# A written order of 3,557 steps, written anew: pooled attention and a two-layer MLP on one core

## The chip, the core and the metric

The kernel runs on one core of a Trainium2 chip. The core has five engines that run side by side, each through its own instruction list in order: TensorE (PE in the profile, with its weight loads as PEld), VectorE (DVE), ScalarE (ACT), GpSimd (POOL) and SyncE (SP), which here only issues DMA transfers. Engines wait for each other through semaphores. The metric is the device time of one execution, in microseconds (us), from its start to its end.

## What is computed

The reference pools the queries by two, runs an ordinary softmax attention for 4 batches of 8 heads (1152 keys, 576 pooled queries, head size 64), and sends the result, as 2304 tokens of 512 numbers, through two dense layers with a leaky ReLU between them:

```
q_pool = q.reshape(B, H, S // 2, 2, D).mean(axis=3)
scores = (1 / sqrt(D)) * q_pool @ k.T
attn   = exp(scores - max) / (sum + 1e-9)
x      = (attn @ v), heads side by side       # 2304 x 512
h      = x @ w_in                             # 512 x 2048
out    = maximum(0.01 * h, h) @ w_out         # 2048 x 512
```

The inputs q, k and v are 32-bit floats; the two weight matrices come as 64-bit floats.

## The kernel before

The work is cut into 3,557 steps, each of one to some tens of instructions on one engine, named by their function and their place: `qk` 9 2 is the third piece of the first score product of head 9. There are 32 heads and, for the dense layers, 9 blocks of 256 tokens.

**One head** goes through this chain. The keys are loaded and turned over on TensorE (`load_k`, `k_tr`), and split into a rounded part by ScalarE (`k_hi`) and a rest by VectorE (`k_lo`); the queries are loaded into one buffer that all heads share (`load_q`, four DMAs), summed in pairs on GpSimd (`q_sum`), turned over and split likewise. `qk` computes rough scores, and `vmax` (line 476, on VectorE) takes their maxima out of the accumulation banks; a bank pair is free for the next product only when its `vmax` is done. `vneg`, `m_tr`, `m_cp` and the DMA step `m_dma` (line 496, tile mt) turn the maxima into a row. `qkt` (line 511) computes the exact scores minus the maximum in nine pieces; two bank pairs take turns, and each is freed by its `exp` on ScalarE (line 515). `pv` multiplies with the values, GpSimd adds up the sums (`esum`, line 525), and `norm` copies the result out of its bank into one of two buffers x1, on ScalarE or VectorE. The sums go the long way round: `r_cp`, the DMA step `r_fold` (four DMAs), `r_inv` on VectorE, the DMA steps `r_row` and `r_wide`, the multiplication `scale` on GpSimd (line 591) and the DMA step `x_out` (line 597, into xd). The buffer x1 of head 8 is the one of head 6, so `norm` 8 waits until the DMAs of `x_out` 6 have landed.

**The weights** come in 32 pieces of 128 x 512. The 64-bit numbers are made into 32-bit ones by `w_f32` in three steps: step 0 on ScalarE (line 619), step 1 on VectorE (line 622, a shift) and step 2 on VectorE (line 625, a shift of one SBUF operand, or-ed into a second one). `w_hi` and `w_lo` then split each piece. All this lies between 41 and 300 us, while heads 2 to 15 are at work. The dense layers (`l1`, `post`, `l2`, and for the later blocks a scheme with fewer products, `g_...`, `l2s`, `o_mix`) fill TensorE beside the later heads and alone at the end.

**What sets the order.** The string ORDER has one letter for each step; `run` goes through it, and each letter takes the next step of its family. So each engine's instruction list is the order of the letters. While `run` goes through the letters, it keeps a reckoning of when each engine is free, from prices written at each `step`. The reckoning chooses two things only: which engine does a step that may go on either of two, and which of several free buffers it takes. `lock=True` in a step on VectorE or GpSimd makes the reckoning hold the two engines apart: such a VectorE step is not begun there before GpSimd is done with its own, nor the other way round. Prices come from `dve`, `act`, `gp` and the like, functions of the number of columns: `dve(512, 2)` is 0.40 us and `dve(512)` 0.66 us. Neither the prices nor the locks put any instruction into the kernel.

Of the kernel before, what the change touches and what calls it, by code (L numbers as in the profile page):

```python
# [18 lines left out]

ND = 3  # L20
# [27 lines left out]
    "43)-244355BB%-43!4.3.4(*+3,53+6,-A.443-../7433B45)0631A4DDD9-E8(EE*6.-!4+,2+),-..BCCF#BCCA$:6%3CF(-34;8-..433!"
    "-.44.53/&-53<55GH440.31-F-4A73.3C9-544.G23.5-H45.553-4=:3.G4&*+.;D,#$+34>6<3,4E&DD/3704AEF35%-1-643HF?.9-84B)E"
    ".3-.2B3(4453-G35.-:.454.A.3/!4=*+,)#$H;5%+A364,#$%5>3D3447B0G!31<E9?CFF-4-6G82..-.G34BA3-3-43..44-3=3../:5*H4;"  # L50
    "5++C3,5>64(CC60DA41-,3-DDEF?EE.8.4-.33<#5)B=2&445H!3-45F7A$.3*+4(+6>-,5,-..?95%A6583F-4.7934.3B/:40-B;GGDD133."
    "-#)4433&$.!-42<3.4%43-3!43.-.4B455.5/A3*+,#6G6=:U;+5$C554>C,0%33A<14A-(74E35.45342H-335).-44&33=49*?55+.-(+,F."
    ":64->-,H3..587G3?443./06D1D4E;EE3A-F39F844&!G)2-343..-3-44G3.34F55<U:*++.D;=B(,,3CC>64AG<?653E&)5A-48=5344B-#."
    ".3*./$(%+>DE,?7401#2D-ER696$!+.3A8),%AB-34-4334:4..-34.-.34-5B(555555;-...A3S4&/7T3U39B<-40*).4+,+1FC,&--F-VVV"
    "VV..V-W...6FGCCG2/:U03G3=C14B4#;<(3356DDEEDE44X3$3F4554734!%3>G2=#B49$&DEC>34536?4A%53*4538H-+4.Y,+6:,33-;455A"
    "7.H3-4V?V49-8.-..U5VVV)<5-AUF3C.V4BVV.GC/01=U3-DVV24E!VHFV3>W646?GH5X3W3:.DE-U484-33.U-4U4.35455;<3*#4V.VVVV$+"
    "+%YV,,3-FF55.GXWG(XA4-V&..YVVVVV/D0EA-!=WB3124.34#-U63.$554%5>C3F-H?46F73.9-434B5G34HD8BD5:.-3-43E4..).3*Z/ZYZ"
    "+FUECCC4&HGZZZZZZG;+DEFF,ZZ[VBUV<VA,GVVVZGB3DDEUE5A=550WZV1VCFGFGCZVXZDE4XYZ52HVVV>&36WU[4?3FGBD-E3.54X463548Y"
    "3U479A:;34(F3G--VCVDVVVV<EZWYXYZZF=4ZZZZ..G-)5--ZZZZZ.Z..3[!.>?(/01*4ZZZ5+5255+,,#55553A$!4%[634-347.3349RS#T-"
    "$%648.3)3UU4U-U-.VVV5555VUVVVVV:VVVWVVVUU.54U3W*&AX+V(+VVYAZ5]W&ZXYX4YVVVV,,A-)-345..VVWZ./&;Z03<XY-!.1-4.ZZZ]"  # L60
    "2=-.*>6+,+,34ZUU-3.[347(634-3?9448-:;<55.U3434=../35555036124>4733#44A9$336%4434-?ZV:85.)5555---VV.Z&(;V&V.V.*"
    "++-.,,-.Z./<Z=>)ZZZWAZ[304!X5531#34A$24356%3443*4+?+73-5Y,,6(5)4394.-38-43..43-.534!4-UUVV:;VVVVVU55VVVV5A-UUA"
    "WVW..5X.VVVVYVVWUARX/#Y012UUX3YZZZZZZZZ$6[344S%354*34<=T6>535+U+?3,,454789&-3VV-4-.(..-VV!ZVUV.A:Z#WA$3;-.Z4Z)"
    "555--.Z.ZZVV%.34<-/01V(ZVV.V[3-.6W=>?42343-4753.!3-U4&.63-55.49U43.435:;<4/5*85555)]535013442=76>93++,3X44,#$:"
    "3*+A,+%6,54X-?-YYAVVVVVV5.;53<8W4.-.34!-555334#4.-.A-Z$.VX.A%UYUZV/V3-&(&.VVVZ4W-.=-.0Z5XZZY)ZZ1-553556]45[.23"
    "3-4.743434-../601334UU4>9*33+(44)6+34,5,55555?234*+8733,6+4554343!:;<=4>,#$93ZVVVVA4%--.V.UV?ZZ8--WX.-YUV.&VV."
    "VV!Z3-#$4..VW/55AAZU55Z0%13XY(--..)4VVZVVV52U3!45-Z[V-3.6W:3;<=.-.4344&73#*45$+U3+6>9%AX43?4,,-3A85434.!-3:./."
    "0Y1;#(-4.7ZV9VVV$%V--..2555555:3VZ<=ZZWXYZZZZ6);-<4[34.334*UA3+6+U,,44R-=34553>5?475..U/013!3>A8ST-54462.343?-"
    "693.44:34;-558.555]-334.-4(3U34-VVVV.)..A/V<&V5=&(74W3*+4+5056619,2,3344#$>34?:)8X*(AA55ZUU5Z)Z5;V5%!++,,AVZ3-"
    "<Z-43Z..-4--.ZZ.VVVV-WU[3.3.#4.Y43/!$0VV4555VVVV31=4-W%6234X>3.74-55534934&6?3.5X8-344UU.-3.3-4534-VVVVVYVWVVY"  # L70
    "..VZZ.5555Z#U/U54*++0A$VXVUYVW5ZZZ:;1A,ZZ%ZZZZZZZZ,II<2L[A6NP-JK[M3374OQ4II.3&3-46359=>.-4XN34?84-345553555.45"
    "5.-Y3.-VV:&.JV.P4VVVWXUU5YU/01UV;OL2VVVVVVVVVWVVW364343463XX344QK<79M3I3=>R?SU87443344U6IP6TVVUVVVUVVVVNJYYKOL"
    "QV:;VMI55ZVUVVUVVVZZZ5UUVVVVVVIPR<ZVZZ^Q95UNZ:5[UVVLUVVV555VV7IIMUU^Z_LMZZOZZZPQV^V=UZVZ]]V_VVVVVVJK>SJU9I:`?a"
    "`a[^__8VVUVVUUUbIbNONOJ`;;TV^_VV`<<VVVaKVVVaUILMbI^b`a_UU^=V>V=VVVVVVUVV`PaV^VUVVVU>b?KQIILMVLMJKVNO^JKPUUQNOb"
    "^PVVVVVVVQV?VVUR___`ab`abcbccbbS^^^`TUUa_VVVVVUcUVVVV^VVVVb`VUU^aV^VUUVVVVVVVVVVVU__bUcccVUVVVV_Vc`V_Va_^_UUbV"
    "`UaVVVVbV``aVVa`VbVbUU`aabb^^VVVbVVV^bb^^]d_U__URVVVVVcc_ccccU`aVUUVVVST`VVVVVVcbUUUc`UVVVVVVVVaab^`a^VVVVUVVV"
# [1001 lines left out]
```

## Time and profile before

| | us |
|---|---|
| three runs of the kernel before | 897.91, 898.41, 903.2; median 898.41 |
| the profiled execution | 897.51 |
| its span, from the first to the last instruction | 895.7 |
| TensorE busy | 861.3 |
| VectorE, GpSimd, ScalarE busy | 524.2, 494.3, 390.4 |

The span is 1.8 us shorter than the profiled execution; what lies around it is the same for any order of the work. A row of the trace gives the start of a group of like instructions in us from the start of the span, how long the group lasted, the engine, the line, the operation and its operands, how many instructions it holds, and in brackets the idle time of the engine before it and what ended that.

### The profile page before, as it was taken

How to read it: one execution, taken by the hardware profiler on the slowest of the kernel's cores; microseconds unless marked ns; L12 is line 12 of the kernel's file. 1: busy time of each engine (PE TensorE's matmuls, PEld its weight loads, DVE VectorE, ACT ScalarE, POOL GpSimd, SP SyncE). 2: the span in 40 equal slices, each digit the busy share in tenths (PEclk: the TensorE clock that was granted, in tenths of full speed). 3: DMA queues.
4: the chain of work that ended last, by engine and by line, in shares of the span. 5: the costliest groups of instructions: out<-in, count | busy, mean ns of one | idle time of the engine just before them, and what ended most of it. 6: DMA issues, size and time to landing. Idle time of an engine off the chain costs nothing.

```text
span 895.7 us, 19761 instructions
## 1 busy us (share of the span) xinstructions
PE 861.3 (96%) x7736; PEld 693.0 (77%) x7736; DVE 524.2 (59%) x813; ACT 390.4 (44%) x706; POOL 494.3 (55%) x400
## 2 busy tenths in 40 slices
...
GB/s 207 214 175 209 171 166 152 173 203 202 256 245 195 107 252 172 115 194 160 131 146 110 146 130 150 129 191 109 117 180 247 205 247 256 197 267 177 242 143 48
DMA packets 107309, 159.74 MB, mean 178 GB/s; under 512 B 25856, under 2 KB 74304, under 8 KB 107216
## 3 DMA queue, kind: packets, MB, share of 16 engines
...
q8 instruction: 61, 1.00, 0.5%
...
## 4 chain that ended last, share of the span: by engine, by line
PE 81%; DMA 6%; DVE 6%; SPq 2%; issue 2%; ACT 2%; POOL 0%; DVEq 0%; ACTq 0%; POOLq 0%
PE banks L690 22%; PE banks L511 17%; PE banks L537 13%; PE banks L781 11%; PE banks L461 4%; PE banks L822 3%; PE banks L824 3%; PE banks L823 3%; DVE stat L476 2%; DMA rt<-rs 2%; PE banks L553 1%; DMA ws<-wd 1%; DMA raw<-in_moe_w_in_dram 1%; PE banks L548 1%; SPq L571 1%
## 5 line engine op out<-in xcount | busy, mean ns | idle before, releaser
L476 DVE TENSOR_REDUCE stat<-banks 128x1 f32<-128x1024 f32 (+3 forms) x224 | 217.6, 1005 | 113.5 <-PE banks L461 96.7
L515 ACT ACTIVATE e<-banks 128x576 f32<-128x576 f32 x234 | 148.2, 650 | 136.8 <-PE banks L511 120.6
L690 PE MATMUL banks<-xb,ws 128*128 128x256 f32 x1344 | 176.4, 285 | 0.3 <-DMA ws<-wd 0.2
L690 PEld LDWEIGHTS banks<-xb,ws 128*128 128x128 f32 x1344 | 167.4, 190 | 10.2 <-issue 4.8
L525 POOL TENSOR_TENSOR sm<-sm,e 128x576 f32<-128x576 f32 x119 | 171.0, 1454 | 3.4 <-ACT e L515 2.0
L511 PE MATMUL banks<-qh,ka 64*128 64x288 f32 x1152 | 146.5, 330 | 5.9 <-DVE stat L476 4.0
L537 PE MATMUL banks<-e,vv 128*64 128x288 f32 x936 | 139.5, 411 | 0.1
L511 PEld LDWEIGHTS banks<-qh,ka 64*128 64x128 f32 x1152 | 93.9, 191 | 52.6 <-issue 18.6
L537 PEld LDWEIGHTS banks<-e,vv 128*64 128x64 f32 x936 | 70.0, 136 | 50.6 <-issue 7.0
L511 PE MATMUL banks<-mt,hot 64*128 64x288 f32 x576 | 89.8, 297 | 2.2 <-DMA mt<-ms 2.2
L511 PE MATMUL banks<-ql,ka 64*128 64x288 f32 x576 | 88.1, 296 | 0.0
L591 POOL TENSOR_TENSOR x<-x,rs 128x288 f32<-128x288 f32 x32 | 27.0, 846 | 99.9 <-DMA rs<-rd 86.5
L461 PE MATMUL banks<-ka,qh 64*128 64x512 f32 (+1 forms) x320 | 69.4, 445 | 6.4 <-ACT ka L256 2.2
L511 PEld LDWEIGHTS banks<-mt,hot 64*128 64x128 f32 x576 | 58.1, 189 | 3.3 <-DMA mt<-ms 3.1
L781 PE MATMUL banks<-wo,gg 128*128 128x256 f32 x340 | 60.3, 282 | 0.0
L411 POOL TENSOR_TENSOR qs<-qn 112x384 f32<-112x384 f32 x32 | 32.9, 1029 | 49.3 <-DMA qn<-in_q_dram 22.7
L525 POOL TENSOR_TENSOR sm<-e 128x576 f32<-128x576 f32 x32 | 46.1, 1441 | 24.3 <-ACT e L515 24.3
L511 PEld LDWEIGHTS banks<-ql,ka 64*128 64x128 f32 x576 | 57.3, 190 | 0.0
L432 DVE SCALAR_TENSOR_TENSOR ql<-banks,qh 64x288 fp32r<-64x288 f32 x66 | 29.9, 453 | 46.1 <-ACT qh L429 45.3
L703 POOL TENSOR_TENSOR gg<-g,gg 128x512 fp32r<-128x512 f32 x32 | 41.8, 1311 | 22.1 <-DVE gg L256 11.6
L822 PE MATMUL banks<-wo,gg 128*128 128x512 f32 x128 | 53.3, 416 | 0.0
L824 PE MATMUL banks<-wo,gg 128*128 128x512 f32 x128 | 50.9, 398 | 0.0
...
## 6 DMA issues: line engine op xcount, KB each, us to landing
...
qn<-in_q_dram SPq DMA_DIRECT2D x128, 72.0 KB
...
```

Source lines behind the costliest of these rows:

```text
L411: ENG[e].tensor_tensor(out=qs[hd][:n], in0=a, in1=b, op=ALU.add)
L461: nc.tensor.matmul(p[:n, x, :KW], lhsT=qh[hd][r, o:o + n], rhs=kh[r, :KW], start=True, stop=True)
L476: nc.vector.tensor_reduce(out=d, in_=p, axis=AX.X, op=ALU.max)
L511: nc.tensor.matmul(p[:, x, :HW], lhsT=w[r], rhs=m[r, hf * HW:(hf + 1) * HW], start=(n == 0), stop=(n == 3))
L515: nc.scalar.activation(out=ex[hd, u], in_=sps.pop((hd, u))[:, :, :HW], func=AF.Exp)
L525: ENG[e].tensor_tensor(out=o, in0=a, in1=b, op=ALU.add)
L537: nc.tensor.matmul(p[64 * hf:64 * hf + 64, :HW], lhsT=vv[hd][:, t, :], rhs=probs(hd, t, hf), start=(t == 0), stop=(t == KT - 1),)
L690: nc.tensor.matmul(p, lhsT=wst[i, f][:, a, c, :], rhs=xx[i][x][:, c, :], start=(n == 0), stop=(n == 3 * KC - 1))
L703: ENG[e].tensor_tensor(out=t[:, 1], in0=gf.pop((i, fp)), in1=f32(t[:, 0]), op=ALU.subtract)
L781: nc.tensor.matmul(o, lhsT=g[i, p][:, a], rhs=w[:, x], start=(p == 0 and n == 0 and half == 0), stop=(p == FH - 1 and n == 2), skip_group_ ...
L822: nc.tensor.matmul(p, lhsT=gh, rhs=wo[f][:, 0], start=(f == hf * FH), stop=False)
L824: nc.tensor.matmul(p, lhsT=gl, rhs=wo[f][:, 0], start=False, stop=(f == hf * FH + FH - 1))
```

## The change

The change has three parts. First, the whole string ORDER is another one, of the same 3,557 letters, so that every engine's instruction list is in another order. Second, some prices and locks of the reckoning are others: step 1 and step 2 of `w_f32` are reckoned at 0.78 and 1.2 us, the middle step of `post` at 0.75 us on VectorE, each without a lock; step 0 of `w_f32` has 0.06 us more; and a TensorE step that has to wait for more than 1 us in the reckoning is reckoned 1.2 us longer. Third, the `vmax` steps of head 1 now name the step `zeros`, which clears their tile on GpSimd, as one they depend on. A constant W0 is added that nothing reads. Four lines are added, so that line 476 of before is line 480 after, 622 is 626 and 625 is 629.

```diff
 ORDER = (
-    "()*+,++!+,,,!@B(B)#$--%#$.-..*--..-.+.!+,B/0(%)1A-*+,.+B-!.-CCCC2.,3A-34,--.4.34#3../&&3$40A453-(1#%-..B4A3$53"
     ...
+    "!#$%()*++++!#,,,-$%,.-.--..@B()*++B-!-.(A--)..,/01BC..--*,(C2.C.+,+,3434!-.3#)-43$.&.3/440AA3%A1-.B#55-.4!5353"
     ...
 )
@@
-        end = self.free[e] = at + s.eng[e]
+        free, end = self.free[e], at + s.eng[e]
+        self.free[e] = end
         if e == "PE":
+            if at > free + 1.0:
+                end = self.free[e] = end + 1.2
@@
-                step(vmax, hd, y[2], ..., deps=[("qk", hd, n)])
+                step(vmax, hd, y[2], ..., deps=[("qk", hd, n)] + ([("zeros", hd)] if 0 < hd < len(mts) else []))
@@
-        step(w_f32, i, 0, eng={"ACT": act(512)}, deps=[("w_load", i)])
-        step(w_f32, i, 1, eng={"DVE": dve(512, 2)}, lock=True, deps=[("w_f32", i, 0)], takes=[("raw", [("w_lo", i)])])
-        step(w_f32, i, 2, eng={"DVE": dve(512)}, lock=True, deps=[("w_f32", i, 1)])
+        step(w_f32, i, 0, eng={"ACT": act(512) + 0.06}, deps=[("w_load", i)])
+        step(w_f32, i, 1, eng={"DVE": 0.78}, deps=[("w_f32", i, 0)], takes=[("raw", [("w_lo", i)])])
+        step(w_f32, i, 2, eng={"DVE": 1.2}, deps=[("w_f32", i, 1)])
@@
-                step(post, i, fp, 1, eng={"DVE": dve(512, 2), "ACT": act(512)}, lock=True, deps=[("post", i, fp, 0)])
+                step(post, i, fp, 1, eng={"DVE": 0.75, "ACT": act(512)}, deps=[("post", i, fp, 0)])
```

**Place 1: VectorE, from the maxima of head 6 to those of head 7** (stat is written by `vmax`, neg by `vneg`, ql is the query's rest, raw a piece of the weights, rt the sums). Before:

```order
L476 TENSOR_REDUCE stat_66<-banks 64x1
L479 TENSOR_REDUCE neg_68<-stat_66 128x5
L576 TENSOR_REDUCE rt<-rt 96x6
L577 RECIPROCAL rt<-rt 96x6
L432 SCALAR_TENSOR_TENSOR ql<-banks,qh 64x288
L622 TENSOR_SCALAR raw<-raw 128x512
L432 SCALAR_TENSOR_TENSOR ql<-banks,qh 64x288
L622 TENSOR_SCALAR raw<-raw 128x512 x2
L625 SCALAR_TENSOR_TENSOR raw<-raw 128x512 x3
L476 TENSOR_REDUCE stat_67<-banks 128x1 x4
```

With the change:

```order
L480 TENSOR_REDUCE stat_66<-banks 64x1
L626 TENSOR_SCALAR raw<-raw 128x512
L629 SCALAR_TENSOR_TENSOR raw<-raw 128x512
L580 TENSOR_REDUCE rt<-rt 96x6
L581 RECIPROCAL rt<-rt 96x6
L436 SCALAR_TENSOR_TENSOR ql<-banks,qh 64x288
L483 TENSOR_REDUCE neg_68<-stat_66 128x5
L626 TENSOR_SCALAR raw<-raw 128x512 x2
L436 SCALAR_TENSOR_TENSOR ql<-banks,qh 64x288
L480 TENSOR_REDUCE stat_67<-banks 128x1 x3
```

Six steps on weights stood in a body between `vneg` 6 and the first `vmax` of head 7; two shifts stand there now, another pair stands ahead of `vneg`, and the second steps of the two shifts come after the maxima of head 7.

**Place 2: SyncE, from the maxima's row of head 9 to `x_out` 6** (mt is `m_dma`, rd `r_row`, rs `r_wide`, rt `r_fold`, qn `load_q`, xd `x_out`). Before:

```order
L496 DMA mt_73<-ms 1x5x128 x2
L580 DMA rd_84<-rt 96x6
L674 DMA ws<-wd_111 128x1024
L571 DMA rt<-rs 48x1x6 x4
L584 DMA rs<-rd_84 64x288 x2
L608 DMA raw<-in_moe_w_in_dram 128x4x128
L395 DMA qn_70<-in_q_dram 48x3x128 x4
L441 DMA ql<-ql 64x288 x2
L580 DMA rd_85<-rt 96x6
L597 DMA xd_74<-x_2107 64x288 x2
```

With the change:

```order
L584 DMA rd_84<-rt 96x6
L500 DMA mt_73<-ms 1x5x128 x2
L588 DMA rs<-rd_84 64x288 x2
L399 DMA qn_70<-in_q_dram 48x3x128 x4
L451 DMA vv<-in_v_dram 128x576
L644 DMA wd_116<-ws 128x1024
L575 DMA rt<-rs 48x1x6 x4
L601 DMA xd_74<-x_1648 64x288 x2
L601 DMA xd_74<-x_2067 64x288 x2
```

`x_out` 5, which stood five rows above this piece, now stands right ahead of `x_out` 6, and `load_q` and `r_fold` stand ahead of both. On ScalarE `norm` 7, which waits for the one, and `norm` 8, which waits for the other, now have a single `exp` between them.

**Place 3: SyncE, from the start.** Before:

```order
L395 DMA qn_70<-in_q_dram 48x3x128 x4
L366 DMA kn<-in_k_dram 128x576
L367 DMA kn<-in_k_dram 128x64
L366 DMA kn<-in_k_dram 128x576
L367 DMA kn<-in_k_dram 128x64
```

With the change:

```order
L370 DMA kn<-in_k_dram 128x576
L371 DMA kn<-in_k_dram 128x64
L399 DMA qn_70<-in_q_dram 48x3x128 x4
L370 DMA kn<-in_k_dram 128x576
L371 DMA kn<-in_k_dram 128x64
```

The keys of head 0 now go ahead of its queries. Further on, the fourth `load_q` stands ahead of the `m_dma` of head 0, where it stood behind it before.

## Rows read from the trace of the kernel before

**Rows 1.** The page: the span, and TensorE's busy time.

```profile
span 895.7 us, 19761 instructions
PE 861.3 (96%) x7736; PEld 693.0 (77%) x7736; DVE 524.2 (59%) x813; ACT 390.4 (44%) x706; POOL 494.3 (55%) x400
```

**Rows 2.** Windows: stretch, length; busy us (instructions) of five engines; granted clock; DMA.

```profile
0.00:45.00 45.00, 32.74 (x305) 23.44 (x305) 31.79 (x50) 21.90 (x40) 14.92 (x21) 1.00 0.70 211
45.00:270.00 225.00, 209.20 (x2142) 148.41 (x2141) 159.07 (x219) 134.37 (x249) 159.94 (x123) 0.96 0.65 196
270.00:895.70 625.70, 619.35 (x5294) 521.10 (x5292) 333.29 (x544) 234.17 (x418) 319.43 (x256) 1.00 0.55 170
```

**Rows 3.** TensorE's timeline: its waits of over 1 us from 45 to 270 us.

```profile
71.31 0.28 PE L485 MATMUL banks<-ident,neg 64*128 64x64 f32 x2 [1.10 <-DVE neg L479]
...
105.08 0.49 PE L461 MATMUL banks<-ka,qh 64*128 64x512 f32 x1 [1.24 <-ACT x L256]
108.53 0.84 PE L511 MATMUL banks<-qh,ka 64*128 64x288 f32 x4 [2.96 <-DVE stat L476]
...
143.72 0.40 PE L511 MATMUL banks<-mt,hot 64*128 64x288 f32 x1 [1.42 <-DMA mt<-ms]
...
173.49 0.43 PE L464 MATMUL banks<-ka,qh 64*128 64x128 f32 x4 [3.03 <-ACT x L256]
...
266.27 0.39 PE L420 MATMUL banks<-ident,qs 48*128 48x48 f32 x6 [1.73 <-DVE stat L476]
```

**Rows 4.** Windows, as rows 2: the five stretches of half clock.

```profile
106.79:113.60 6.81, 5.07 (x44) 4.16 (x48) 4.56 (x5) 2.41 (x5) 4.53 (x4) 0.50 0.78 259
...
144.30:147.74 3.44, 3.18 (x24) 3.18 (x26) 1.15 (x1) 1.43 (x3) 1.55 (x2) 0.50 0.86 282
...
175.05:178.46 3.41, 3.41 (x40) 1.84 (x36) 3.13 (x7) 1.38 (x4) 1.10 (x1) 0.50 0.77 229
...
195.50:198.95 3.45, 3.45 (x18) 3.45 (x17) 3.26 (x3) 1.14 (x3) 2.59 (x3) 0.51 0.85 289
...
267.21:270.60 3.39, 3.39 (x10) 2.62 (x9) 2.60 (x5) 3.35 (x7) 1.30 (x1) 0.50 0.95 364
```

**Rows 5.** VectorE's timeline, ahead of the waits at 108.53 and 266.27 us.

```profile
101.78 5.44 DVE L625 SCALAR_TENSOR_TENSOR raw<-raw 128x512 uint32<-128x512 uint32 x3
107.25 3.49 DVE L476 TENSOR_REDUCE stat<-banks 128x1 f32<-128x1024 f32 x3
...
262.14 2.85 DVE L625 SCALAR_TENSOR_TENSOR raw<-raw 128x512 uint32<-128x512 uint32 x1
```

**Rows 6.** Groups of VectorE by shape: count | busy us, mean ns | idle before.

```profile
L625 DVE SCALAR_TENSOR_TENSOR raw<-raw 128x512 uint32<-128x512 uint32 x32 | 39.0, 1235 | 0.5
...
L622 DVE TENSOR_SCALAR raw<-raw 128x512 uint32<-128x512 uint32 x32 | 24.1, 773 | 13.8 <-POOL wo L637 8.7 <-POOL ws L637 4.6 <-issue 0.5
```

**Rows 7.** Lines 625 and 622: ns of one, least/median/most.

```profile
L625 DVE SCALAR_TENSOR_TENSOR raw<-raw x32: 659/693/4234, 42.5 to 299.8; 128x512 uint32<-128x512 uint32 x32
L622 DVE TENSOR_SCALAR raw<-raw x32: 381/427/1651, 41.5 to 298.9; 128x512 uint32<-128x512 uint32 x32
```

**Rows 8.** GpSimd's timeline beside the row of 101.78 us in rows 5.

```profile
101.78 1.57 POOL L411 TENSOR_TENSOR qs<-qn 112x384 f32<-112x384 f32 x1 [3.24 <-DMA qn<-in_q_dram]
...
104.67 1.40 POOL L525 TENSOR_TENSOR sm<-e,gg 128x576 f32<-128x576 f32 x1
```

**Rows 9.** SyncE's timeline: DMA issues, start and length of the issuing.

```profile
1.19 1.84 SPq L395 DMA_DIRECT2D qn<-in_q_dram  x4
3.08 0.44 SPq L366 DMA_DIRECT2D kn<-in_k_dram  x1
...
18.47 1.60 SPq L496 DMA_DIRECT2D mt<-ms  x2
...
138.27 3.52 SPq L395 DMA_DIRECT2D qn<-in_q_dram  x4
...
170.33 1.11 SPq L597 DMA_DIRECT2D xd<-x  x2
```

More of the change, by code (lines that the diff above doesn't have):

```diff
@@ L17 @@
 DRAM = bass.MemoryType.DRAM
+W0 = 5
 ND = 3
@@ L46 @@
 ORDER = (
-    "()*+,++!+,,,!@B(B)#$--%#$.-..*--..-.+.!+,B/0(%)1A-*+,.+B-!.-CCCC2.,3A-34,--.4.34#3../&&3$40A453-(1#%-..B4A3$53"
[L48 to L76, printed above, removed]
@@ L77 @@
-    "UVV__RS_b`aVUVbbUVV`U_a^b^_^`VVaVTUUUb`aVVVVVVVVb^ddcbbccc_b__VVVVUVV`aV`UUVc^^cccV_Ub_VVUVVVVVVVU`VabVVV^`aUU"
-    "VVVVUUbVVVV^V`VabVVa`aUVV_`b_b`aaVd^^U_`VVbVbbb^^_b`dUVVUUV^VVVVVVUVcccccaabUVVVVb^UVVUVVVV__`V`_a_ccb^c_ab`ab"
-    "`^_a`a`abbbdddcbbbbccbbbbbcccbbbccddd"
+    "!#$%()*++++!#,,,-$%,.-.--..@B()*++B-!-.(A--)..,/01BC..--*,(C2.C.+,+,3434!-.3#)-43$.&.3/440AA3%A1-.B#55-.4!5353"
+    "$42%43-43434-BB(..3&*455++34,,A536-&34D45DD)5.-.7.354EE-B3/.64A0193-8B.*4(+6#+FA,,--C$C2)EBC..634-%3438-4.354:"
@@ new lines @@
+    "!;3..-/0341-7.&.<-4F9.33-4A45.G53B-2B434-3.3545#3.4*().DE++4=,G6/C,:;$3&43>4%5F7A013--D4EC.6!934!-.34<?8.2B-.H"
+    "343:-43-3.4*.AH#4=.+$,55555G+%(A3,/;FFAG<64D#$E33>754-4!%9-0.163F55CCC-.?4G348.-.H2343-3G-...44)=!B33*436+DE+4"
+    ">:64;H,/C01(DA<-?D,83--.55555..F5434&3)=#423-$6A%-..4*>-H..+6+,7E(F,393?BA-4GC87&3B43)/B9:.0-4D4!1GD32543.4-3."
+    "#43;-&3.<$4%43-4.3-34.545*+.E,H+#,3($556/4=53%4AE3EA4-016FFFU!:.->)B55534-723.53.-94G43434.*+3+4C-;(?BA<.,,863"
+    "3-.B44G33:&.A5G555/=;4A)74DE0->3<1-2..963F44--CC6=3.4.(D3&H*34DG>:EE4F3+??;!,63+,84-D83<)4A.-43.3.GD/445#55*++"
@@ new lines @@
+    ",UEF70$16=(5A#$,B%GE>-2%.-633.?&98-.-4344)5553.-A4!33.-..R4(-4U.3S4A7-T93.5:3-.-44*BVV)FFGVVG./B:V++C&,0D1B5E5"
+    "-2;,V66;CCCW.3F344H-.345G<3./D<4#0&AA13$437=34=5>9X5%E>!3D4#4234F36$%434*H3BG:;+5,6455-?DU3?ECC8+,48U79-3.C4-V"
+    ".<VVF5H3.Y-E4(VVV-.U3=-V5A45GFGW!VVA3.../H04VD1)VV3H2-EB4>?663W34XUU.XDEUUD4-85.-343-4334554555..#*V(VV++,A$YE"
+    "Y,VVCV3-%.-FGVVVFCWGX..!V/4VV0-W.1Y33#4&&H$4-.FD2B6%BX3553C4-E6B4C.D-34.B37493455555-HE.534343-ZZZZZZFFGGGCDDD"
+    "C:EEE:.BZZZ;5AHZFFF.GZZZZUG[VVVUD4VEH3<U/05F)CGGZ1Z[4VU=2DEFVUVVVVVB>V*WX++YG3W,6453;34X4,5A-C536DE34Y344?8<57"
@@ new lines @@
+    "B3&.-.V=U>VZV4VVVZC3-YFG9?WZDEZZ.-48AX-Y-FGRZ:!(;.)<ZZZZZZZ=5.*../++#S(0T)51ZZ!A>$Z52[,,6%34555555[&-347UU.334"
+    "4?#3$%946833-44-VVVVUVVUVVVVV..UU---WVVVV.VVXWAV:]YX.U../3505W*ZXUY;VZYVVZV1+V+V(4A,-,.-WXY.3ZZ&4ZZZ-<&2.3465["
+    "U35=>5435-)4!557933?U.4*+64+83,3-5544:;,.-3437.<U3=A.49/A0(1>46)6234#$3%?ZZZ:-!4A8;-..-.ZZ<ZZ&Z-[3=434.*+,>555"
+    "55U3-V?(V+VVUVVVVVUU),4VWV5555V.W-3X43..#4/013$43465*2%3Y+,+,63434A873A-43X94-4.3455534.:Y-3-.VVVVVVV.UA-;-!.W"
+    "XVVV4<5VVW355Y()#=../0ZZ$Z&Z%XYZZ1UZRZ>62[35S443743*+,4+A,3T634?5535()9-!8U.-:;<U44VVAVV&VV5555-.W=X>.--A&ZZ.Z"
@@ new lines @@
+    "ZZVZ.3-#$.4Z./ZVV01%3554--[UUVVVW(..36234434-7.35549-.63?-83-44UU:...343*/455!35501+;5+3XYY72<=44A)6&U,,6334#$"
+    "4%9>VV?VV8!-VVVV5*+-.34+AAV,5,AVVV35WW5-344..-33#5.4--4ZZ5Z.../Z:$%0-XY;ZXZYZZU5!(5]1.[-33U54)642U.3-5<43=(7.4"
+    "59:355-.-6.3;-44.34<>.3]5554579/0134?3*++638,4=23:),4A4*3++4346,33>,?(4)4#$3AA8V54!VV-5553%-;<=U4>U.V.VV--W-.X"
+    "?ZZZZ.Z.ZZ34#A-3../VV5$55!%V4-0-.1VZ[VVVVUVY.&&VVVWX--&.62.3-.WX3474355*U(4U#+YYU96+,3,$%34-45!8A..-.:343U#4&5"
+    "33$57%6-A5)4/4091:.VVVVV555-5-VZWZX;<;YZZZZZ.=R<>Z23.[-343.44*++33554,6,-.S435535A.7=44/>0(?12&93434!-6T34.553"
@@ new lines @@
+    "-46855:;?.553344<=-8-.A3434)-3(.3-4V..VVVV4.V7/W0*314>66+)+555,?239,5843:4*++,#,53]$%;55]ZZ4UZ34A-.-!.VV5Z3--4"
+    "VUUVV.ZZZ.Z(U34-XV<-W3[4U55U...3#43/A5550VVVVV1$YV524W]!65=%3XX344#$34>)%A37A643?-94834Y-3..3UU:&&;Y4<-3-4VVVV"
+    "VVVVVWU..U--.II.UZV.55&XVVY=W55/*01+55+>?,2AL5P,ZZZZZQXAZZNZZZOJKMZZZYZ4ZI6[[3U3-4.734359:;<64344-38.-.4=533I-"
+    "434-VV.VV.VP-V..VVV545VVW55QUU/0VV5V5VXYJ5KVVV51WL2N3W6OXX433MI44I63NJRS4>UUU3K479337449::3T34466VVOUVVVVV5LPQ"
+    "MZVY;<ZZIRI=VVVVZPQNUUUVVLOVJVVKMIIZPUUVVY5QVVVV>ZJZ?N^555555ZZZ;?VVVV[UVV^LSUOVVVV8UV8VV_7MIZNZKIL^JOMP_QUUVV"
```

8 lines of the change are left out of this document (7 added, 1 removed).

## The prediction

> **What bounds the kernel.** The page comes first: TensorE is busy for 861.3 us of a span of 895.7 [rows 1]. The same matmuls are issued before and after, so a new order can only give back time in which TensorE waits, or runs at half its clock. Where that time lies is read next, from windows [rows 2]. In the first 45 us TensorE idles for 12.3, from 45 to 270 us for 15.8, and in all the rest for 6.4, part of it behind the last matmul. The granted clock tells the same: 0.96 in the middle stretch, 1.00 after it. From 270 us on the kernel is bound by TensorE, and another order has nothing to win there. What can be won lies ahead of 270 us.
>
> In that stretch TensorE's own timeline shows six waits of over 1 us [rows 3]: 1.10, 1.24, 2.96, 1.42, 3.03 and 1.73, together 11.5 of the 15.8. The windows of low clock [rows 4] show what follows: after five places where TensorE had stood still or stuttered, the granted clock is 0.50 (1.2 GHz in place of 2.4), once for 6.8 us and four times for 3.4. TensorE is busy there for 5.07 + 3.18 + 3.41 + 3.45 + 3.39 = 18.5 us. At full clock the same matmuls would take about half, so the half clock costs 9.2. The stretch loses 15.8 + 9.2 = 25.0 us in all, and that is the most this change could bring there.
>
> **Who causes the waits.** Two kinds have to be kept apart. The wait of 2.96 ended with a `vmax` on VectorE. That engine had been in three second weight steps, 5.44 us, and came to the maxima of head 7 only at 107.25 [rows 5]. The wait of 1.73 stands behind one such step of 2.85 us [rows 5]. That of 1.10 was ended by VectorE too, and in the cold stretch at 195.50 VectorE is busy for 3.26 of 3.45 us [rows 4]. With half of the cold time at these places (2.5, 1.7 and 1.7) VectorE's lateness costs 2.96 + 2.5 + 1.73 + 1.7 + 1.10 + 1.7 = **11.7 us**. The waits of 1.24 and 3.03 were ended by ScalarE's copy of a head's result (x), which itself waits for an `x_out` to land; that of 1.42 by the maxima's row (mt). With their cold time (1.6 behind 1.42, 1.7 behind 3.03) these three cost 1.24 + 3.0 + 4.7 = **8.9 us**. They are waits for DMA chains.
>
> **Why VectorE was late.** The reckoning behind the old order had 0.40 and 0.66 us for the two weight steps; 32 of each make 33.9 us. They took 773 and 1235 ns on average [rows 6], 64.3 us. So 30.4 us of VectorE's time were not in the plan, and they cost TensorE 11.7 us, 0.385 us for each. The new prices make 63.4 us.
>
> **The change, term by term.** The sum is made against the profiled execution, 897.5 us.
>
> *VectorE's waits.* At place 1 the three second steps no longer stand ahead of the maxima of head 7, only two shifts do, and the one body of six that I find in the new list (pieces 25 to 27) stands beside eight `l2` steps that wait for no `vmax`. For this alone I would take back most of the 11.7. But the new prices are means of two things. Of the 32 second steps 20 took about 0.69 us, the median [rows 7], and 12 took 1.43 to 4.23; of the first steps 19 took about 0.42 and 13 more than 0.6. The long ones lie beside GpSimd: the three that took 5.44 us ended when GpSimd, at work without a pause from 101.78, was done with its third instruction at 106.07 [rows 5, 8]. So a long second step is 2.14 us on average ((39.5 - 20 x 0.69) / 12), 1.45 more than a short one, and a long first step 1.29, 0.87 more. The old reckoning kept these steps and GpSimd's apart, and 12 or 13 of 32 met all the same. The new one doesn't keep them apart, and GpSimd is busy for 159.94 of 225 us, 71% [rows 2]. I take the middle between 39% and 71%, 55%: five more long steps of each kind, 5 x (1.45 + 0.87) = 11.6 us. The time not in the plan is then 64.3 + 11.6 - 63.4 = 12.5 us, which at 0.385 costs 4.8. **Gain 6.9.** Bounds: no more meetings than now, 0.9 us unplanned, gain 11.4; meetings at 71% (11 and 10 more, 24.7 us, 25.6 unplanned), gain 1.8. The middle is a choice: the old plan cannot have been without effect, since 39% is far below 71%, but it was not kept either.
>
> *Waits for DMA chains.* The wait of 1.42: `m_dma` 8 stood behind the four DMAs of a `load_q`, whose issuing took 3.52 us [rows 9]; in the new list they stand behind it, but a `w_load` and four DMAs of `r_fold` stand ahead. Gain between 0 and 3.0, I take the middle, **1.5**. The wait of 1.24 keeps its cause: `norm` 4 is still on ScalarE, behind the same `x_out` 2. The wait of 3.03: at place 2 the old `x_out` 6 was issued at 170.33 [rows 9] and `norm` 8 held ScalarE until it had landed. In the new list `x_out` 5 and 6 go out together, behind ten DMAs (a `load_q`, a load of values, a piece of weights and an `r_fold`), and `norm` 7 can now hold ScalarE as well. `r_wide` 6 stands a little earlier against TensorE's work, which speaks the other way. Between -4.7 and +4.7, I take **0**. Elsewhere the order is new, and a new wait of this kind can come up anywhere; `norm` 10, say, goes from VectorE to ScalarE, where `exp` stands behind it. Nothing of before can show one, so it is bounded by the largest of its kind: 0 to 4.7, I take half, a **loss of 2.4**.
>
> *The start.* At place 3 the keys' two issues, 0.44 us each, go ahead of the queries, so the queries are there 0.9 us later, and the shared query buffer passes that on to the next heads. Against this the keys are turned over while TensorE would wait for queries. The four issues of the fourth `load_q` (1.84 us, by the first one) now stand ahead of `m_dma` 0, which was issued at 18.47 [rows 9] and on which the first exact scores depend. Together 0 to 2.7; I take a **loss of 1.5**, since part of either is covered by `qk` of head 1. The named dependence on `zeros` costs nothing: that step stands behind the first `q_sum` and is long done when head 1 has maxima.
>
> *The rest.* Behind 270 us TensorE is covered; the last transfers end as before: 0, within 0.5.
>
> Sum: -6.9 - 1.5 + 0 + 2.4 + 1.5 = **-4.5**, so 893.0 in the terms of the profiled execution. The three runs' median, 898.41, lies 0.9 above that execution, which makes **893.9 us**. With the bounds the case reaches from 886 to 901.
>
> **Rivals.**
> 1. *The waits go altogether.* Weight steps spread out, no more meetings with GpSimd, the clock never falls, and the waits of 1.42 and 3.03 are gone: 11.7 + 3.0 + 4.7 - 1.5 for the start = 17.9, so 880.5 us. For it speaks that a late VectorE is behind the dearest wait; against it that GpSimd's 71% stays. Chance 0.14.
> 2. *GpSimd takes the gain.* Without the locks, three in four weight steps run beside GpSimd: 12 more long second steps and 11 more long first ones are 27 us, 27.9 are unplanned, and VectorE's waits still cost 10.7 of 11.7. With the other terms (+2.4) that is +1.4: 899.8 us, no change. For it speak the 4.23 us that one step took, and that the list sets no distance between the two engines. Chance 0.21. The Trainium skill states it as a rule ("SBUF — State Buffer", section "SBUF: two separate sides"): VectorE and GpSimd share one pair of ports under an exclusive lock, and a VectorE instruction with two SBUF inputs that meets a GpSimd one waits for all of it. By that rule a step has no mean price, and the trace agrees, with 0.69 us alone and up to 4.23 beside GpSimd.
> 3. *Slower: ScalarE held by `norm`.* Two buffers for results mean that a `norm` waits for the `x_out` of two heads before; ScalarE works in order, so each `exp` behind it waits too, and TensorE has two bank pairs of scores and then stops. One such wait cost 4.7. If three new ones come (`norm` 7 ahead of 8, 9 and 10 are all on ScalarE, each close behind its `x_out`), that is 14.1, with the start's bound of 2.7 and less the 6.9 won +9.9: 908.3 us. It decides from the point where `x_out` lands more than some 3 us after ScalarE reaches the `norm`. Against it: `norm` 3 to 9 stood on ScalarE before, and two waits of over 1 us came of it. Chance 0.11.
>
> The forecast has 0.54. That the new prices change nothing but two choices of engine and buffer is no rival of its own, since the written order is what is changed.
>
> **How the numbers follow.** What a measurement of this kernel can tell from no change is about 1%, 9 us: faster is below 889.4, slower above 907.4. Faster: nearly all of rival 1 and a fifth of the forecast, 0.24. Slower: most of rival 3 and a little of rival 2, 0.10. The rest, 0.66, is within 1%. The range leaves out rival 1 and the worse half of rival 3, and takes in the forecast and rival 2: 883 to 905.
>
> **What would show it.** Right: no body of second weight steps right ahead of maxima, fewer than five stretches at granted clock 0.50, idle time of 45 to 270 us down from 15.8 to about 11. The mean of line 625's steps (629 after) tells the first rival from the second: near 1.2 us, or near 1.8. Waits of TensorE ended by "ACT x" near heads 7 to 10 would show the third. The first 45 us should idle for 12 to 15 us. It would be wrong altogether if TensorE's busy time behind 270 us changed.

## The result: slower, outside the range

The changed kernel takes **913.06 us** (median of four runs, 909.65 to 917.01), the kernel before 898.16 in the same comparison: a ratio of 1.0150 with a 95% interval of 1.0108 to 1.0192, some 13.5 us. Forecast were 893.9 us and a range of 883 to 905. The profiled execution of the changed kernel took 917.0 us.

The page of the changed kernel answers to [rows 1], its windows to [rows 2]:

```profile
span 915.2 us, 19740 instructions
PE 868.0 (95%) x7736; PEld 699.3 (76%) x7736; DVE 534.3 (58%) x804; ACT 397.0 (43%) x716; POOL 502.0 (55%) x399
```

```profile
0.00:45.00 45.00, 30.66 (x273) 21.51 (x273) 31.92 (x43) 19.73 (x36) 18.95 (x24) 1.00 0.66 190
45.00:270.00 225.00, 202.88 (x2048) 144.32 (x2050) 172.45 (x214) 123.64 (x231) 147.69 (x113) 0.94 0.62 179
270.00:915.20 645.20, 634.50 (x5417) 533.46 (x5413) 329.96 (x549) 253.65 (x451) 335.39 (x264) 0.99 0.56 172
```

TensorE's idle time is the length of a stretch less its first figure: 14.3, 22.1 and 10.7 us, where it was 12.3, 15.8 and 6.4. Its busy time rose by 6.75 us with the same 7,736 matmuls, and the clock explains most of it. The windows of low clock answer to [rows 4]:

```profile
48.00:51.40 3.40, 3.40 (x18) 1.93 (x20) 2.19 (x4) 0.65 (x1) 0.00 (x0) 0.51 0.04 10
85.60:89.00 3.40, 3.09 (x24) 3.00 (x26) 2.95 (x4) 0.96 (x2) 0.00 (x0) 0.50 0.84 274
116.30:119.70 3.40, 3.35 (x29) 2.80 (x28) 1.45 (x2) 2.23 (x5) 1.67 (x2) 0.50 0.29 83
150.40:153.80 3.40, 3.40 (x30) 2.45 (x24) 1.29 (x2) 1.06 (x2) 1.63 (x2) 0.51 0.59 121
...
252.80:259.60 6.80, 6.10 (x52) 5.95 (x53) 4.13 (x5) 2.78 (x5) 3.53 (x3) 0.50 0.43 144
413.30:416.70 3.40, 3.40 (x19) 3.40 (x18) 1.49 (x3) 0.00 (x0) 3.40 (x3) 0.50 0.14 27
sum 30.60, PE 29.50 PEld 24.96 DVE 16.52 ACT 11.34 POOL 11.62; mean PE 3.69 PEld 3.12 DVE 2.06 ACT 1.42 POOL 1.45
```

Eight stretches at half clock, busy for 29.5 us, stand against five and 18.5; at full clock the same matmuls would take about half, so 5.5 of the 6.75 us are the clock's, an estimate from these sums. One stretch lies at 413 us, where the prediction saw nothing to lose. What stands ahead of them is in TensorE's own timeline (start, length, line, operands; the idle time before the row and what ended it in brackets):

```profile
47.05 0.49 PE L465 MATMUL banks<-ka,qh 64*128 64x512 f32 x2 [2.63 <-DVE stat L480]
...
84.78 0.50 PE L465 MATMUL banks<-ka,qh 64*128 64x512 f32 x2 [3.21 <-DVE stat L480]
...
115.38 0.50 PE L465 MATMUL banks<-ka,qh 64*128 64x512 f32 x1 [1.78 <-ACT x L260]
...
149.49 0.50 PE L465 MATMUL banks<-ka,qh 64*128 64x512 f32 x2 [2.99 <-DVE stat L480]
...
253.50 0.79 PE L465 MATMUL banks<-ka,qh 64*128 64x512 f32 x1 [1.44 <-DVE x L260]
...
411.36 0.50 PE L465 MATMUL banks<-ka,qh 64*128 64x512 f32 x2 [1.78 <-DVE stat L480]
```

Three waits of about 3 us, at 47, 85 and 149 us, end with a `vmax`; [rows 3] have one. Take the second. VectorE and GpSimd ahead of it, each in its timeline:

```profile
75.69 0.82 DVE L391 TENSOR_TENSOR ka<-banks,ka 128x640 fp32r<-128x640 f32 x1
76.43 5.36 DVE L626 TENSOR_SCALAR raw<-raw 128x512 uint32<-128x512 uint32 x1
81.82 1.77 DVE L629 SCALAR_TENSOR_TENSOR raw<-raw 128x512 uint32<-128x512 uint32 x1
```

```profile
75.95 2.80 POOL L529 TENSOR_TENSOR sm<-e 128x576 f32<-128x576 f32 x2
78.72 2.78 POOL L529 TENSOR_TENSOR sm<-sm,e 128x576 f32<-128x576 f32 x2
81.58 1.46 POOL L529 TENSOR_TENSOR sm<-sm 128x576 f32<-128x576 f32 x1
```

A single shift, 0.43 us where nothing disturbs it [rows 7], takes 5.36. It ends at 81.8, 0.3 us after GpSimd has done four additions in a row (81.5), and the second step ends at 83.6, 0.55 us after the fifth (83.04). The maxima stand behind both. Over the kernel, by line and form (busy us, mean ns of one):

```profile
L629 DVE SCALAR_TENSOR_TENSOR raw<-raw 128x512 uint32<-128x512 uint32 x32 | 44.2, 1394 | 0.5
L626 DVE TENSOR_SCALAR raw<-raw 128x512 uint32<-128x512 uint32 x32 | 37.7, 1194 | 10.6 <-POOL wo L641 5.1 <-POOL sm L529 2.9 <-POOL ws L641 2.4
...
L260 DVE CAST gg<-g 128x512 fp32r<-128x512 f32 x9 | 12.1, 1343 | 1.4 <-ACT g L702 1.3
```

Against [rows 6] the second step rose from 1235 to 1394 ns and the shift from 773 to 1194: 82.8 us for 64 steps (32 times each mean), where it was 64.3. The third row is a kind of step that the prediction left out: the cast of a result (`post`, step 1), which also lost its lock. One of them explains 413 us. VectorE, then GpSimd:

```profile
405.19 4.98 DVE L260 CAST gg<-g 128x512 fp32r<-128x512 f32 x1
410.09 2.34 DVE L480 TENSOR_REDUCE stat<-banks 128x1 f32<-128x1024 f32 x2
```

```profile
403.09 2.79 POOL L529 TENSOR_TENSOR sm<-sm,e 128x576 f32<-128x576 f32 x2
405.83 1.29 POOL L707 TENSOR_TENSOR gg<-g,gg 128x512 fp32r<-128x512 f32 x1
407.08 2.81 POOL L529 TENSOR_TENSOR sm<-sm,e 128x576 f32<-128x576 f32 x2
```

A cast, of 0.42 us where it is shortest in these runs, lasts until GpSimd has done its row, TensorE then waits 1.78 us for the maxima behind it, and the clock falls.

Losing the lock did not make the casts longer on average. The kernel before, with the lock in its reckoning, has 13 of them on VectorE with a mean of 1387 ns, and one is longer than any here:

```profile
377.61 6.75 DVE L256 CAST gg<-g 128x512 fp32r<-128x512 f32 x1
```

TensorE has no wait in the 7 us behind it: the next VectorE step is the low half of some keys, and maxima come only at 387.93 us. What differs is what stands behind a cast.

### The profile page after: what moved, and what is told of

Same layout as the page of the kernel before. It is cut to its first block, busy times and chain, and to the rows that moved or that the text cites. A ratio compares the mean times of both kernels' runs of the same rounds, so it can differ in the third digit from the quotient of the medians.

```text
span 915.2 us, 19740 instructions
## 1 busy us (share of the span) xinstructions
PE 868.0 (95%) x7736; PEld 699.3 (76%) x7736; DVE 534.3 (58%) x804; ACT 397.0 (43%) x716; POOL 502.0 (55%) x399
## 4 chain that ended last, share of the span: by engine, by line
PE 73%; DVE 9%; DMA 7%; issue 3%; SPq 3%; POOL 3%; ACT 1%; DVEq 0%; POOLq 0%; ACTq 0%
PE banks L694 21%; PE banks L515 14%; PE banks L541 11%; PE banks L785 11%; DVE stat L480 4%; PE banks L465 4%; PE banks L826 3%; PE banks L827 3%; PE banks L828 2%; DVE raw L629 2%; PE banks L552 1%; DMA xd<-x 1%; DVE raw L626 1%; POOL sm L529 1%; DMA mt<-ms 1%
## 5 line engine op out<-in xcount | busy, mean ns | idle before, releaser
L515 PE MATMUL banks<-qh,ka 64*128 64x288 f32 x1152 | 151.2, 334 | 6.1 <-ACT e L519 2.0
L515 PEld LDWEIGHTS banks<-qh,ka 64*128 64x128 f32 x1152 | 98.7, 195 | 50.1 <-issue 17.0
L515 PE MATMUL banks<-mt,hot 64*128 64x288 f32 x576 | 94.0, 302 | 1.1 <-DMA mt<-ms 1.1
L465 PE MATMUL banks<-ka,qh 64*128 64x512 f32 (+1 forms) x320 | 72.6, 451 | 22.1 <-DVE stat L480 12.8
L515 PE MATMUL banks<-ql,ka 64*128 64x288 f32 x576 | 92.5, 302 | 0.0
L515 PEld LDWEIGHTS banks<-mt,hot 64*128 64x128 f32 x576 | 62.4, 195 | 2.1 <-DMA mt<-ms 2.1
L515 PEld LDWEIGHTS banks<-ql,ka 64*128 64x128 f32 x576 | 61.1, 195 | 0.0
L465 PEld LDWEIGHTS banks<-ka,qh 64*128 64x128 f32 (+1 forms) x320 | 31.4, 184 | 37.6 <-DVE stat L480 15.3
L785 PE MATMUL banks<-wo,gg 128*128 128x256 f32 x268 | 54.2, 282 | 0.0
L391 DVE TENSOR_TENSOR ka<-banks,ka 128x640 fp32r<-128x640 f32 x32 | 26.3, 822 | 45.0 <-ACT ka L260 44.6
```

The lines of the kernel that those rows point to most:

```text
L465: nc.tensor.matmul(p[:n, x, :KW], lhsT=qh[hd][r, o:o + n], rhs=kh[r, :KW], start=True, stop=True)
L515: nc.tensor.matmul(p[:, x, :HW], lhsT=w[r], rhs=m[r, hf * HW:(hf + 1) * HW], start=(n == 0), stop=(n == 3))
L785: nc.tensor.matmul(o, lhsT=g[i, p][:, a], rhs=w[:, x], start=(p == 0 and n == 0 and half == 0), stop=(p == FH - 1 and n == 2), skip_group_ ...
```

## The experiments

**Theory:** the weight steps on VectorE, which read and write SBUF alone, wait for GpSimd's unbroken work, and the new order puts more of them beside it and ahead of maxima. **Rival:** the new order has other waits (transfers, the start), and long steps only lie beside them. Each order was run with and without the suspected meeting.

**Weight steps that do not meet GpSimd.** The two steps become reductions over an axis of length one, of the same lone length; the weights' bits are then not put together.

```diff
-            nc.vector.tensor_scalar(out=t, in0=y, scalar1=3, ..., op0=ALU.logical_shift_left)
+            one = f32(y).rearrange("p (n o) -> p n o", o=1)
+            nc.vector.tensor_reduce(out=f32(t)[:, :256], in_=one[:, :256], axis=AX.X, op=ALU.max)
@@
-            nc.vector.scalar_tensor_tensor(out=t, in0=w[:, :, 0], scalar=29, in1=t, ...)
+            one = f32(y).rearrange("p (n o) -> p n o", o=1)
+            nc.vector.tensor_reduce(out=f32(t), in_=one, axis=AX.X, op=ALU.max)
```

In the new order: 

> The changed kernel with the two weight steps on VectorE replaced by two reductions of the same length (256 and 512 columns, one SBUF operand, nothing reduced), so the bits of the 64-bit weights aren't put together and the output is not the reference's. Theory (weight steps are held by GpSimd): the mean of the two steps falls from 1194 and 1394 ns to about 400 and 670, none is over 1 us, the waits ended by VectorE go with the half clock behind them, and the kernel takes 886 to 894 us. Rival (the new order is worse in itself, its start, its DMA chains, TensorE's sequence): 905 us or more, and 10 us or more over the old order with the same replacement.

In the order of before: 

> The old order with the same replacement of the two weight steps by reductions (weights not put together, output not the reference's). Theory (GpSimd holds the weight steps): the 11.7 us of VectorE's waits go, 884 to 890 us, within 5 us of the new order so treated. Rival (the order itself): about 893 to 898, and 10 us or more below the new order so treated.

Measured: new order **899.76 us**, ratio 1.0013 [0.9992, 1.0034]; old order **891.49**, ratio 0.9911 [0.9884, 0.9939], both against the kernel before. The steps in the new order:

```profile
L631 DVE TENSOR_REDUCE raw<-raw 128x512 f32<-128x512 f32 x32 | 21.3, 679 | 0.5
...
L627 DVE TENSOR_REDUCE raw<-raw 128x256 f32<-128x256 f32 x32 | 12.7, 410 | 13.3 <-POOL wo L641 8.7 <-POOL ws L641 2.4 <-issue 1.9
```

The longest of them took 421 and 689 ns (421 and 693 in the old order), so no reduction waited for GpSimd. The meeting of these 64 steps was worth 1.0150 - 1.0013 = 0.0137, 12.3 us, in the new order and 8.0 in the old. Both prices hold what GpSimd lost by the meeting too: its busy time fell by 7.1 us in the new order and by 6.1 in the old, so that side hardly tells the orders apart. Both times fall between what theory and rival had for them: the two orders still lie 8 to 9 us apart, so this was not all.

**The casts too.** In the profile of the new order without long weight steps the wait for maxima near 396 us was still there, 1.81 us behind a cast of 5.02. So the casts on VectorE became reductions as well; over an axis of length one such a reduction is a copy.

```diff
-            copy(e, gg[i, fp][:, 0]..., gf[i, fp])
+            to = gg[i, fp][:, 0]...
+            if e == "DVE":
+                nc.vector.tensor_reduce(out=to, in_=gf[i, fp].rearrange("p (n o) -> p n o", o=1), axis=AX.X, op=ALU.max)
+            else:
+                copy(e, to, gf[i, fp])
```

In the new order: 

> The changed order, with the two weight steps on VectorE replaced as before by reductions of the same lone length (the weights' bits are not put together) and now also the nine casts of a result (post, step 1), which become reductions over an axis of length one, that is copies. No step between SBUF and SBUF of these three kinds then meets GpSimd. Theory (GpSimd holds the casts as it held the weight steps; one cast ended 5 us late at 410 us, ahead of maxima): casts 680 ns in place of 1955, the wait near 396 us gone, 896 to 898 us. Rival (casts stand where TensorE has work): 899 to 901, as without them.

In the order of before: 

> The same three replacements in the order of the kernel before (weights' bits not put together). Theory: that order keeps the casts where nothing waits for them, 890 to 892 us, as with the weight steps alone (891.5). Rival: 888 to 889. The distance between this and the changed order with the same replacements is what the new order itself costs: 5 to 7 us if casts were part of it, still 8 if not.

Measured: **896.41 us**, ratio 0.9974 [0.9954, 0.9994], and **892.55 us**, ratio 0.9950 [0.9923, 0.9976]. In the new order the casts were worth 0.0039, 3.5 us, give or take 2.6 by the two intervals; in the old nothing that shows (its two ratios overlap). The two orders now lie 2 to 4 us apart, less than was expected even if casts were part of it. Windows of the new order without the three kinds of meeting:

```profile
0.00:45.00 45.00, 31.90 (x287) 22.79 (x289) 31.86 (x50) 20.20 (x37) 19.39 (x25) 1.00 0.67 193
45.00:270.00 225.00, 210.63 (x2172) 150.03 (x2169) 142.64 (x225) 133.56 (x249) 155.65 (x123) 0.98 0.67 198
270.00:894.10 624.10, 615.83 (x5282) 519.58 (x5280) 307.00 (x531) 242.92 (x432) 319.21 (x253) 1.00 0.55 171
```

Idle time from 45 to 270 us is 14.4, the clock 0.98, and behind 270 us 8.3 are idle. A finer measure is the time at which TensorE has done the same share of its matmuls, counted at their full-clock length. The changed kernel is behind the one before by 2.5 us at 32 us, 7.6 at 55, 15.8 at 274 and 18.1 shortly before the end. With both orders freed of the meetings, the new one is behind the old by 2.7 us at 32 us, within 3 us of it either way from there to 260 us, and behind by 3.0 shortly before the end. Of the excess of 18 us in these profiles 15 hang on the three kinds of step, and about 3 are left. The start alone brings as many by 32 us, but between 150 and 240 us the lag is gone for stretches and then comes back, so the last 3 us are not shown to be the start's. By the medians 13.5 us split into 7.8 to 11.3 for the meetings and 2.2 to 5.7 for the rest, the ends given by the two measurements of the old order; the interval of the 13.5 itself goes from 9.7 to 17.2.

**The start, mended three ways.** First, head 0's first maxima ahead of the low half of head 1's keys (`%`) and of the last low half of the queries (`,`), and `m_dma` 0 ahead of the fourth `load_q`; engines and buffers of all steps stay those of the changed order:

```diff
+    ("!#,,,-$%,.-.--..@B", "!#,,,-$.%,-.--..@B"),
+    ("..--*,(C2.", "..--*,C2(."),
```

> The changed order with its start mended: the first maxima of head 0 stand ahead of the low half of head 1's keys and of the fourth low half of the queries on VectorE, and the exact scores' row of head 0 (m_dma 0) goes out ahead of the fourth load_q on SP. Buffers and engines of every step stay those of the changed order. Theory (the start costs some 2.5 us, which TensorE never gets back since it is the bound from there on): first vmax at about 11 us in place of 12.5, m_dma 0 at about 18.5, TensorE's lag at 30 us nearly gone, 910 to 911 us in place of 913. Rival (later waits swallow the lag, as they wait for VectorE and not for TensorE): 912.5 to 914.

Measured: **913.81 us**, ratio 1.0179 [1.0145, 1.0214]. No gain, and the trace shows why: the first maximum came at 11.31 us in place of 12.51, but the low half of the keys holds the banks of the next products, and TensorE now waited 3.2 us for it, where it had waited 1.9. The row went out at 20.63 us, where it had at 20.34. TensorE's waits in the first 20 us (total, times, longest):

```profile
PE banks L492 <- DVE ka L418: 3.2, 1, 3.2
PE banks L451 <- POOL stat L433: 2.5, 1, 2.5
```

Second, without the three meetings, head 1's keys turned over only behind head 0's first four products (`"!,,,-,.-.--..#$%@B"`), the row still ahead of `load_q`:

> The changed order with the three kinds of step off the port (weight steps and result casts as reductions; the weights' bits not put together), and its start mended in another place than in a_start: head 1's keys are turned over on TensorE only behind the first four products of head 0, with their high and low halves behind head 0's first four maxima, and the exact scores' row of head 0 goes out ahead of the fourth load_q. In a_start TensorE waited 3.17 us for the low half of head 1's keys, since it holds the banks that the next products need. Theory (what is left between the two orders without the port, 896.4 against 892.6, is that start): the wait for the keys at 10 us gone, no lag behind the order of before at 30 us, 893 to 894.5. Rival (the few us are waits for transfers further on): 896 to 897.

Measured: **896.03 us**, ratio 0.9966 [0.9950, 0.9982], the same as without the edit. The wait for the low half is gone, and TensorE waits 2.72 us for maxima instead, from 12.64 us on; the row went out at 20.87, where without the edit it had at 19.72. Third, only the queries of head 0 loaded and summed ahead of the keys again (`"()!#$%*++++!#"`):

> The changed order with the three kinds of step off the port (the weights' bits not put together), and one thing of its start undone: the queries of head 0 are loaded and summed ahead of the keys again, as in the kernel before; all else of the start stays. Read from the trace: with keys first GpSimd's sum of the queries began at 5.76 us here and at 4.76 in the kernel before, and the exact scores' row went out at 19.72 against 18.47. Theory (the loads' order sets the start): the sum at about 4.8 us, the row at 18.7, 1 us less lag at 30 us (1.7 in place of 2.7), 895 to 896 us. Rival: the two other heads' banks set it, and the row goes out no sooner than 19.5; time as without it, 896 to 897. The time alone can hardly tell these; the row's issue can.

Measured: **895.64 us**, ratio 0.9965 [0.9947, 0.9984]. GpSimd's sum began at 4.79 us, as the theory had it, but the keys came later, TensorE's list has them first, and the row went out at 20.11, so the rival holds:

```profile
6.38 0.80 PE L405 MATMUL banks<-ident,kn 64*128 64x64 f32 x10 [6.38 <-DMA kn<-in_k_dram]
```

Each of the three took one wait of the start's chain away and met the next. That the start brings 2.5 to 2.7 us of lag by 32 us is read from the traces; which of its changes have to be undone together, and whether the lag would then be won at the end, stays open.

**GpSimd made to wait instead.** All work is done here: the GpSimd instruction that comes next in written order behind a weight step waits for that step (`asked` collects the weight steps issued since the last one), so that GpSimd leaves a gap.

```diff
+    class Yielding:
+        def tensor_tensor(self, **k):
+            i = nc.gpsimd.tensor_tensor(**k)
+            for x in asked:
+                tc.add_manual_dep(i.ins, x.ins.name, ..., reason="yield")
+            asked.clear()
```

In the new order: 

> The changed kernel, all its work done, in which each GpSimd sum or product that comes next in the written order after a weight step of VectorE waits for that step. Theory (a weight step waits until GpSimd has a pause): no weight step lasts over 2.3 us, the steps of 5 us are gone, the time falls from 913 to 896 to 904 us. Rival (order itself): no gain, 910 us or more; GpSimd's own waits could make it slower.

In the order of before: 

> The kernel before, all its work done, with the same waits of GpSimd for the weight steps. Theory: the steps of 2.8 and 4.2 us are gone, and with them the waits of 2.96 and 1.73 us and their half clock: 890 to 896 us. Rival: 898 or more, since GpSimd, late by its waits, holds up the sums.

Measured: new order **908.94 us**, ratio 1.0099 [1.0069, 1.0128]; old order **894.10**, ratio 0.9935 [0.9909, 0.9960]. The old order's time is where the theory had it, the new one's between theory and rival. In the old order the second step's mean falls from 1235 to 695 ns, its lone length, the shift's only from 773 to 657 (alone 427). In the new one they stay at 936 and 716 ns, since a step can meet GpSimd work that was written ahead of it, and GpSimd's own lateness comes up as a new wait. GpSimd, then TensorE, in the new order:

```profile
280.55 1.40 POOL L258 TENSOR_TENSOR sm<-e,kn 128x576 f32<-128x576 f32 x1 [2.50 <-DVE raw L643]
281.91 2.49 POOL L258 TENSOR_TENSOR wo<-raw,wo 128x512 fp32r<-128x512 f32 x2
```

```profile
283.85 1.43 PE L708 MATMUL banks<-xb,ws 128*128 128x256 f32 x5 [2.92 <-ACT raw L274]
```

GpSimd stands for 2.50 us behind three second steps, ScalarE's evacuation behind GpSimd, TensorE behind that.

**Both mends together.** GpSimd waits for the weight steps and the casts are reductions, with nothing left out, in the old order and, with the second mend of the start, in the new:

> A version meant to be used: the order of the kernel before, GpSimd's next instruction in written order behind a weight step waits for that step, and the casts of results on VectorE are reductions over an axis of length one. Nothing is left out. Theory: the 894.1 us of the version with the waits alone, less what the casts cost, 891 to 893.5. Rival: 894 to 895, no further gain.

> The changed order with all its work done and everything mended that the runs have named: GpSimd waits for the weight steps, the casts are reductions over an axis of length one, the start as in a_start2. Theory: the version with GpSimd waiting gave 908.9; less 3.4 for the casts and 2.5 for the start, 902 to 904, still above the order of before, since a GpSimd that waits for a late VectorE costs something of its own (a wait of 2.9 us at 281 us). Rival: 893 to 897, the new order then no worse than the old.

Measured: old order **892.09 us**, ratio 0.9942 [0.9919, 0.9964]; new order **906.01 us**, ratio 1.0072 [1.0045, 1.0098]. The first is faster than both kernels, but not told apart from the waits alone (0.9935): the casts of the old order cost nothing, as above. The second lies between its theory (902 to 904) and no gain (908.9): the mend of the start brought nothing in the run above either, and the wait of 2.92 us behind GpSimd is still there, at 283.37 us. The version of the old order, by line:

```profile
L639 DVE SCALAR_TENSOR_TENSOR raw<-raw 128x512 uint32<-128x512 uint32 x32 | 22.2, 711 | 0.5
L636 DVE TENSOR_SCALAR raw<-raw 128x512 uint32<-128x512 uint32 x32 | 19.5, 631 | 17.5 <-POOL wo L254 11.0 <-POOL ws L254 6.5
```

## Why the prediction was wrong

**The step that failed is "the time not in the plan".** The prediction took the priced 63.4 us off the steps' 75.9, charged only the 12.5 left over, and so made VectorE's waits a gain of 6.9. But a price in the reckoning doesn't hide a step: it only places the next letters by a mean, and no step takes the mean. What costs is the time over the lone length, 35.8 us for the 64 steps by the medians of [rows 7]: 28.5 us before and 47.0 after. The experiments price it: 12.3 us for 47.0 is 0.26 in the new order; in the old 8.0 or, by the second measurement, 4.5 for 28.5 is 0.28 or 0.16. These are averages; that the cost grows evenly with the time is not shown. With the forecast's own 75.9 us, 11.6 over the old, 0.26 makes a loss of 3.0, where the term said a gain of 6.9. This one credit is 10 of the 19 us between forecast and result. What it was taken from was too large as well: VectorE's lateness was put at 11.7 us in the old order, and without the meetings that order gained 8.0 or 4.5.

**Its sizes.** The number of meetings was nearly right, their length was not: 17 long second steps and 18 long first ones were expected, 16 and 19 are there (from 0.98 and over 0.7 us). But a long step was put at 2.14 and 1.29 us, the means of the old order, and four steps of the new one take from 5.06 to 6.26. These four hold 20.0 of the 47.0 us; all others together come to 27.0, less than the 28.5 of the old order. So the 11.6 us more that were expected became 18.5. The sign was there: the longest second step of [rows 7], 4.23 us, is one of the three of [rows 5]; it ended at 106.62 us, 0.55 behind the third of the GpSimd instructions of [rows 8], and the prediction averaged it with the others. Why the old order had no weight step over 4.23 us is not shown.

**The rest behind 270 us, put at 0 within 0.5,** was the second failure. It rested on TensorE's being covered there, and the casts were not looked up: 3.5 us by the runs, though three of the nine stand ahead of 270 us. Idle time behind 270 us rose from 6.4 to 10.7 us and a stretch at half clock came up at 413 us. The test named for it, TensorE's busy time behind 270 us, was a poor one: it rose by 15.2 us, but TensorE also works off there what it is behind by at 270 us.

**The start**, a loss of 1.5 with 2.7 as bound, came out near the bound: 2.5 us of lag at 32 us. The queue's part was seen; the low half of head 1's keys between the queries and the first maxima was not. Nor was the clock. The windows give 1.00 for the first 45 us, but in the changed kernel a pair of `qk` products takes 0.80 us at 17.27 us, as long as one at 253.50 in a stretch of half clock, and 0.49 at 47.05. The same ten products tell when that ends, in the kernel before:

```profile
25.72 0.74 PE L375 MATMUL banks<-ident,kn 64*128 64x64 f32 x10
29.80 0.47 PE L375 MATMUL banks<-ident,kn 64*128 64x64 f32 x10
```

and in the changed one:

```profile
28.05 0.73 PE L379 MATMUL banks<-ident,kn 64*128 64x64 f32 x10
32.32 0.47 PE L379 MATMUL banks<-ident,kn 64*128 64x64 f32 x10
```

So both kernels begin at the lower level, and the changed one leaves it later: pairs of `qkt` products shorten from 0.44 to 0.30 us at 28.3 us before, and from 0.49 to 0.30 at 31 us with the change. What this adds to the lag, and whether it is cause or effect, was not separated.

**The transfers** came out about as put. At place 2 `norm` 7 and 8 started with no idle time of ScalarE, and "ACT x" comes to 2.4 us in three waits. TensorE waits for the maxima's row 1.1 us in all, and a new wait of 1.71 us for keys goes from 219.93 to 221.63, right ahead of a stretch at half clock. **Rival 3** forecast the right sign and nearly the time, 908.3, by a mechanism that did not occur: that was luck. **Rival 1** is refuted from another side: without the meetings of these kinds of step the old order takes 891.5 to 892.6, so 880.5 was out of reach for this cause.

**The range.** The 886 to 901 "with the bounds" is less than the bounds give: added up, they reach from about 879 to 909. The measured 913 lies outside that too, and no choice within the bounds would have led there. By the estimates above some 10 us of the miss are the credit, 1.8 the steps' length at 0.26, 3.5 the casts, 1.0 the start; the 3 that are left lie within the interval of the comparison.

**Rival 2 had the mechanism.** It stopped at no change because it too took off the priced time. The mean of the second steps, its test against rival 1, came out at 1.39 between the two, and the shift's mean, which was not in the test, moved more. The Trainium skill ("SBUF — State Buffer", section "Who interferes with whom") names casts and `tensor_scalar` steps among those that can contend with GpSimd for one pair of ports and says that a reduction never contends on this chip. The traces agree on all three, with 4.98 us for a cast, 5.36 for a shift, and 410 and 679 ns for the reductions. It says that the loser waits for the whole instruction. Of the 40 long steps of the changed kernel 33 end behind the first GpSimd instruction that they meet; the shift at 76.43 us waited through four.
